# Top-k softmax with the exponentials taken before the comparison, FFN weights kept unsplit, and a shorter list of early expert work

## The chip, the cores and the metric

One NeuronCore of a Trainium2 chip runs the whole program. The metric is the time of one execution in device microseconds; it was measured three times before the change.

## The reference, cut to what matters

```python
def _attn_ref(q, k, v):                       # 2 batches, 8 heads, 576 tokens, head size 64
    scores = scale * np.matmul(q, k.transpose(0, 1, 3, 2))
    kth = np.partition(scores, -32, axis=-1)[..., -32:-31]
    scores = np.where(scores >= kth, scores, -1000000000.0)
    attn = np.exp(scores - np.max(scores, axis=-1, keepdims=True))
    attn = attn / (np.sum(attn, axis=-1, keepdims=True) + 1e-09)
    return np.matmul(attn, v)

def _moe_ref(x, w_in, w_out):                 # 1152 tokens, 512 wide, 2048 hidden
    h = x @ w_in
    return (h * (1.0 / (1.0 + np.exp(-h)))) @ w_out

def _moe2_ref(x, w_gate, w1, w2):             # 8 experts, 1024 hidden, all of them on all tokens
    P = np.exp(x @ w_gate - (x @ w_gate).max())
    for _ in range(8):                        # Sinkhorn: rows, then columns, normalised
        ...
    for e in range(8):
        out += P[:, e:e+1] * (np.maximum(x @ w1[e], 0.0) @ w2[e])
```

The output of the attention feeds the first FFN, and that feeds the experts. The first FFN's weights arrive as 64-bit floats.

## The kernel before, in words

**Tiles.** The 1152 tokens are nine token tiles of 128, numbered 0 to 8. The attention is done in five groups of token tiles: [0], [1, 2], [3, 4], [5, 6], [7, 8]. A group is made of units, one or two for each of the four head pairs. A unit has score tiles of 128 queries by 576 keys: one for each head and query block, and "h" tiles in which half of the rows belong to one head and half to the other. There are 72 score tiles (64 and 8 h).

**A score tile** (`score_tile`, L276). Four matmuls of 288 columns: two with the high part of q against all 128 rows of `kk` (which holds the high and the low part of k), two with the low part of q against the 64 rows that hold k's high part. ACT copies the scores to `s`. VectorE then finds the 32 largest of each row: four MAX8 (L295) with three MATCH_REPLACE8 (L300) between them. ACT computes Relu(kth - s) (L303), VectorE overwrites what lies below the kth with a large negative number (COPY_PREDICATED, L304), ACT takes the exponential with its row sum (L305), VectorE forms the reciprocal of the sum (L306, L307), and GpSimd scales the row (L308). TensorE transposes the row (L311, L313) and multiplies with v (L322).

**The FFN on one tile or two.** Group g's tokens go through the first FFN as m0 (tile 0), m1 (tiles 1, 2), m2 (tiles 3, 4), and m3 (tiles 5 to 8, after all attention). m1 to m3 run over 16 blocks f of 128 hidden values. A block computes `hidden` (12 matmuls), the activation, and `product` (six matmuls of 512 columns with two token tiles), each value in a high and a low part of reduced 32-bit precision, three matmuls for each full product. In m1 and m2 the activation after ACT's tanh (L398) is four GpSimd instructions: t (L402), g (L403), gH (L416), gL (L417). m0 works with whole 32-bit weights in four blocks of 512.

**Splitting.** A weight block of 128 by 512 is split by one ACT copy (L127) and one subtraction (L128), on GpSimd unless said otherwise. While m0 runs, each of its 32 weight blocks is converted from 64 bits (`narrow`, L444 to L449), split once, and written to HBM in split form (`kept_in`, `kept_out`); m1 to m3 load the split form and need no split.

**Early expert work.** The eight experts on nine token tiles are 72 pieces. The list `FILL` has some of them done early, between the FFN's parts: after m0 five experts on tile 0, after m1 experts 0 and 1 on tiles [1, 2], after m2 expert 2 on [1, 2] and experts 0 and 1 on [3, 4]. These results go to HBM and are added later. "split" treats each of an expert's eight blocks as above, "half" splits only the first weight and runs the product in one whole 32-bit pass, "split+half" alternates. What is left runs after the Sinkhorn iterations, in units of up to four token tiles.

**What sets the order.** Each instruction gets a priority (`tc.cur_priority`; units of the attention count up in steps of GAP), and a scheduler puts every engine's instructions in one fixed order at build time. The engines and the DMA queue of SP then run in that order. Buffers are shared by pools: three `wa` and four `wb` weight tiles (`wap`, `wbp`), five score tiles (`SB`). Groups 2 and 4 put their attention output into the same `x` tile, groups 1 and 3 into another.

## Time and profile before

| | us |
|---|---|
| three runs | 1337.5, 1337.9, 1342.37 (median 1337.9) |
| the profiled execution | 1342.67 |
| its span, first to last instruction | 1340.8 |

| engine | busy us | share of the span |
|---|---|---|
| TensorE (PE) | 1263.8 | 94% |
| VectorE (DVE) | 703.5 | 52% |
| ScalarE (ACT) | 552.5 | 41% |
| GpSimd (POOL) | 428.0 | 32% |

The shares are means over unlike stages. The attention lasts until the last reciprocal at 522.5 us; in that time VectorE is nearly always at work. From then to about 613 us the rest of the early expert work runs, with m3 from 591 us. From 690 us on TensorE runs experts alone. PE's busy time counts matmuls that overlap, so a PE that is busy all of the time may still be working at less than its best pace; the distance from one start to the next tells the pace.

### The profile page before, as it was taken

To read this page: it belongs to the slowest core of one execution; us is meant where nothing else is said; L and a number is where in the kernel's file an instruction comes from. 1 tells how busy PE (TensorE), PEld (TensorE's weight loads), DVE (VectorE), ACT (ScalarE), POOL (GpSimd) and SP (SyncE) were. 2 spreads that over 40 slices of the span, in tenths; PEclk is the share of its full clock that TensorE was granted. 3 is DMA by queue.
4 is the path that set the end of the run, shared out by engine and by line. 5 is a ranking of instruction groups with operands and counts; after the bars stand their busy time and mean duration, and the time that the engine had idled before them with its cause. 6 is when DMAs were issued, how large, how long until landed. Compare 5 with 4: busy or idle time off the path is not lost.

```text
span 1340.8 us, 18725 instructions
## 1 busy us (share of the span) xinstructions
PE 1263.8 (94%) x6563; PEld 994.6 (74%) x6563; DVE 703.5 (52%) x1489; ACT 552.5 (41%) x1169; POOL 428.0 (32%) x475
## 2 busy tenths in 40 slices
PE   3579989999999999989999999999999999999998
PEld 2344545578768887768979879889888888888887
DVE  5999989989999985022233541232231331323332
ACT  4879745655667566542231231131131221313221
POOL 2768411146557787970010130020020110202110
PEclk9979889999899999999999999999999999999999
DMA  6999977797445864577520250040030120313210
GB/s 172 274 316 333 289 245 223 226 291 242 131 122 165 290 211 120 149 242 251 187 72 8 67 162 0 7 119 1 16 118 0 47 79 9 104 31 113 76 33 32
DMA packets 159725, 186.91 MB, mean 139 GB/s; under 512 B 34320, under 2 KB 110864, under 8 KB 159632
## 3 DMA queue, kind: packets, MB, share of 16 engines
q1 hardware_dynamic: 159632, 185.72, 44.8%
q8 instruction: 52, 0.85, 0.3%
q14 instruction: 41, 0.34, 0.1%
HBM read 153.63 MB, written 23.07 MB: 132 GB/s over the span
## 4 chain that ended last, share of the span: by engine, by line
PE 53%; DMA 2%; POOL 2%; issue 1%; DVE 1%; ACT 0%; DVEq 0%; SPq 0%; ACTq 0%; POOLq 0%
PE h L135 9%; PE h L137 9%; PE h L136 9%; PE y L135 7%; PE y L137 7%; PE y L136 7%; DMA yk<-ky 1%; PE bank L137 1%; PE bank L135 1%; PE bank L136 1%; POOL wa L128 1%; PE y_m L136 1%; PE y_m L137 1%; PE y_m L135 1%; POOL wb L128 1%
## 5 line engine op out<-in xcount | busy, mean ns | idle before, releaser
L410 ACT ACTIVATE gH<-h 128x512 fp32r<-128x512 f32 (+2 forms) x144 | 73.4, 510 | 384.4 <-PE h L137 381.8
L411 DVE SCALAR_TENSOR_TENSOR gL<-h,gH 128x512 fp32r<-128x512 f32 (+2 forms) x144 | 83.3, 578 | 278.2 <-ACT gH L410 278.1
L128 POOL TENSOR_TENSOR wc<-raw,wc 128x512 fp32r<-128x512 f32 x40 | 52.2, 1305 | 404.6 <-ACT wc L127 404.6
L295 DVE MAX8 m<-w 128x8 f32<-128x576 f32 x192 | 141.6, 749 | 0.4
L128 POOL TENSOR_TENSOR wa<-raw,wa 128x512 fp32r<-128x512 f32 x64 | 82.9, 1295 | 148.5 <-ACT wa L127 146.4
L137 PE MATMUL h<-x1H,wc 128*128 128x512 f32 (+2 forms) x360 | 124.8, 347 | 0.0
L136 PE MATMUL h<-x1L,wc 128*128 128x512 f32 (+2 forms) x360 | 124.8, 347 | 0.0
L135 PE MATMUL h<-x1H,wc 128*128 128x512 f32 (+2 forms) x360 | 124.4, 346 | 0.0
L128 DVE TENSOR_TENSOR wc<-raw,wc 128x512 fp32r<-128x512 f32 x40 | 51.5, 1288 | 120.2 <-ACT wc L127 115.8
L135 PE MATMUL y<-wc,gH 128*128 128x512 f32 x285 | 111.7, 392 | 0.0
L136 PE MATMUL y<-wc,gH 128*128 128x512 f32 x285 | 111.6, 391 | 0.0
L137 PE MATMUL y<-wc,gL 128*128 128x512 f32 x285 | 101.9, 392 | 0.6 <-DVE gL L411 0.6
L300 DVE MATCH_REPLACE8 w<-m,w 128x576 f32<-128x576 f32 x128 | 95.1, 743 | 0.0
L308 POOL TENSOR_SCALAR s<-s,sm 128x576 f32<-128x576 f32 x64 | 47.8, 748 | 104.4 <-DVE sm L307 64.6
L137 PE MATMUL h<-x1H,wa 128*128 128x512 f32 (+2 forms) x216 | 75.2, 348 | 0.0
L135 PE MATMUL h<-x1H,wa 128*128 128x512 f32 (+2 forms) x216 | 75.1, 348 | 0.0
L136 PE MATMUL h<-x1L,wa 128*128 128x512 f32 (+2 forms) x216 | 75.0, 347 | 0.0
L135 PEld LDWEIGHTS h<-x1H,wc 128*128 128x128 f32 x360 | 67.7, 188 | 9.5
L136 PEld LDWEIGHTS h<-x1L,wc 128*128 128x128 f32 x360 | 67.8, 188 | 9.5
L127 ACT ACTIVATE wc<-raw 128x512 fp32r<-128x512 f32 x80 | 46.5, 623 | 65.5 <-PE y L137 45.4
L137 PEld LDWEIGHTS h<-x1H,wc 128*128 128x128 f32 x360 | 67.7, 188 | 7.4
L136 PE MATMUL y<-wb,gH 128*128 128x512 f32 x171 | 67.7, 396 | 0.0
(228 smaller groups left out, 3196.7 us busy)
## 6 DMA issues: line engine op xcount, KB each, us to landing
raw<-in_moe_w_dram SPq DMA_DIRECT2D x196, 256.0 KB, 3.0
wa<-kept_in SPq DMA_DIRECT2D x48, 512.0 KB, 4.3
...
```

Source lines behind the costliest of these rows:

```text
L127: nc.scalar.activation(dH, src, AF.Copy)
L128: eng.tensor_sub(dL, src, dH.bitcast(F32))
L135: nc.tensor.matmul(ps, wH, xH, start=first, stop=False)
L136: nc.tensor.matmul(ps, wH, xL, start=False, stop=False)
L137: nc.tensor.matmul(ps, wL, xH, start=False, stop=last)
L295: nc.vector.max(mr, src)
L300: nc.vector.match_replace(out=w, in_to_replace=mr, in_values=src, imm_value=-3e38)
L308: nc.gpsimd.tensor_scalar(s, s, sm[:, 3:4], 1.0, op0=ALU.mult, op1=ALU.mult)
L410: nc.scalar.activation(gH, ph, AF.Relu)
L411: nc.vector.scalar_tensor_tensor(gL, ph, 0.0, gH.bitcast(F32), op0=ALU.max, op1=ALU.subtract)
```

## The change

The top-k softmax takes the exponential of the whole row into a new tile `e` right after the first MAX8 (the maximum is known then). After the fourth MAX8 one VectorE instruction compares the scores with the kth, multiplies the result with `e`, and gives the row sum. The Relu on ACT, the COPY_PREDICATED and the row sum of the exponential go.

The low part of q is kept in two buffers `qLz` of which the rows of the other head are zero, so that all four matmuls of a score tile have 128 rows; the last chunk of keys of the product with v is likewise 128 rows with zeros in v.

m0's weights are written to HBM as they are (`kept_in`, `kept_out`, half the bytes); all 32 blocks stay in buffers of their own until then. m1, m2 and m3 load them and split them, two splits for a block f: on GpSimd, in m3 the second one on VectorE. The pools `wap` and `wbp` now lie where m0's buffers were.

`FILL` loses expert 2 on [1, 2] and expert 1 on [3, 4]; expert 1 on [1, 2] becomes "split+half".

```diff
-    1: [(0, [1, 2], "half"), (1, [1, 2], "split")],
-    2: [(2, [1, 2], "split+half"), (0, [3, 4], "split"), (1, [3, 4], "split")],
+    1: [(0, [1, 2], "half"), (1, [1, 2], "split+half")],
+    2: [(0, [3, 4], "split")],
...
-    return conv_at(i) + 2 * GAP
+    return conv_at(i) + 4 * GAP
...
-    kept_in = drp.tile([DFF // P, P, 2 * W], F32, name="kept_in")
-    kept_out = drp.tile([DFF, 2 * W], F32, name="kept_out")
+    kept_in = drp.tile([DFF // W, NDC, P, W], F32, name="kept_in")
+    kept_out = drp.tile([DFF, W], F32, name="kept_out")
...
-        nc.sync.dma_start(vn[0:64, :, 4, :], vs[:, 4 * P : S, :].rearrange("h p d -> p h d"))
+        nc.gpsimd.memset(vn[0:64, :, 4, :], 0.0)
+        nc.sync.dma_start(vn[64:P, :, 4, :], vs[:, 4 * P : S, :].rearrange("h p d -> p h d"))
...
+            if n:
+                nc.sync.dma_start(low.bitcast(F32)[r, j, : n * P], qL.bitcast(F32)[r, : n * P])
...
-            low = (qL[r, cols], kk[r]) if len(heads) == 1 else (qL[:, j, cols], kk)
-            for a, c, part in ((qq[:, j, cols], kk, 0), (*low, 1)):
+            for part, a in enumerate((qq, qL)):
...
-                nc.vector.tensor_scalar(sm[:, 0:1], m8[:, 0:1], MASKED, -SCALE,
-                                        op0=ALU.max, op1=ALU.mult)
+                nc.vector.tensor_scalar(sm[:, 0:1], m8[:, 0:1], -SCALE, None, op0=ALU.mult)
+                nc.scalar.activation(e, s, AF.Exp, scale=SCALE, bias=sm[:, 0:1])
...
-        nc.scalar.activation(w, s, AF.Relu, scale=-1.0, bias=m8[:, TOPK - 1 : TOPK])
-        nc.vector.copy_predicated(s, w.bitcast(I32), neg.to_broadcast([P, S]))
-        nc.scalar.activation(s, s, AF.Exp, scale=SCALE, bias=sm[:, 0:1], accum_out=sm[:, 1:2])
+        nc.vector.scalar_tensor_tensor(s, s, m8[:, TOPK - 1 : TOPK], e, op0=ALU.is_ge, op1=ALU.mult,
+                                       accum_out=sm[:, 1:2])
...
-            ws = (wap, wbp)[part].tile([P, 2 * W], F32R, name=f"wab_{i}", tag=("wa", "wb")[part])
-            split(ws[:, 0:W], ws[:, W:], x)
-            if part:
-                nc.sync.dma_start(kept_out[r], ws.bitcast(F32))
...
+            tc.cur_priority = keep_at(i)
+            nc.sync.dma_start(kept_out[r] if part else kept_in[F, c], x)
...
-        nc.sync.dma_start(ws[0].bitcast(F32), kept_in[f])
-        r = slice(f * P, (f + 1) * P)
-        nc.sync.dma_start(ws[1].bitcast(F32), kept_out[r])
+        a = kept_in[f // NDC][:, :, f % NDC * P : (f % NDC + 1) * P].rearrange("c p f -> p c f")
+        load_split(ws[0], a, nc.gpsimd)
+        load_split(ws[1], kept_out[f * P : (f + 1) * P], nc.vector if late else nc.gpsimd)
```

Three places in the engines' fixed order follow. In the rows a name before the arrow is written, names behind it are read; the first number after `t_m2_`, `g_m2_`, `gH_m2_`, `gL_m2_` is the block f.

GpSimd in the middle of m2, from one block's t to that of the block after next, before:

```order
L402 TENSOR_TENSOR t_m2_10_4336<-t_m2_10_4336,hs_m2_10_4338 128x256
L417 TENSOR_TENSOR gL_m2_9_4301<-g_m2_9_4302,gH_m2_9_4300 128x256
L403 TENSOR_TENSOR g_m2_10_4335<-t_m2_10_4336,hs_m2_10_4338 128x256
L416 TENSOR_SCALAR gH_m2_10_4333<-g_m2_10_4335 128x256
L308 TENSOR_SCALAR s_4_1_2_0_0_6334<-s_4_1_2_0_0_6334,sm_4_1_2_0_0_6338 128x576
L417 TENSOR_TENSOR gL_m2_10_4334<-g_m2_10_4335,gH_m2_10_4333 128x256
L402 TENSOR_TENSOR t_m2_11_4369<-t_m2_11_4369,hs_m2_11_4371 128x256
L403 TENSOR_TENSOR g_m2_11_4368<-t_m2_11_4369,hs_m2_11_4371 128x256
L416 TENSOR_SCALAR gH_m2_11_4366<-g_m2_11_4368 128x256
L417 TENSOR_TENSOR gL_m2_11_4367<-g_m2_11_4368,gH_m2_11_4366 128x256
L402 TENSOR_TENSOR t_m2_12_4402<-t_m2_12_4402,hs_m2_12_4404 128x256
```

and the same place after:

```order
L407 TENSOR_TENSOR t_m2_10_4377<-t_m2_10_4377,hs_m2_10_4379 128x256
L408 TENSOR_TENSOR g_m2_9_4337<-t_m2_9_4338,hs_m2_9_4340 128x256
L422 TENSOR_TENSOR gL_m2_8_4297<-g_m2_8_4298,gH_m2_8_4296 128x256
L128 TENSOR_TENSOR wa_262_4508<-raw_263_4510,wa_262_4508 128x512
L421 TENSOR_SCALAR gH_m2_9_4335<-g_m2_9_4337 128x256
L128 TENSOR_TENSOR wb_250_4392<-raw_252_4397,wb_250_4392 128x512
L408 TENSOR_TENSOR g_m2_10_4376<-t_m2_10_4377,hs_m2_10_4379 128x256
L407 TENSOR_TENSOR t_m2_11_4416<-t_m2_11_4416,hs_m2_11_4418 128x256
L128 TENSOR_TENSOR wb_254_4431<-raw_256_4436,wb_254_4431 128x512
L422 TENSOR_TENSOR gL_m2_9_4336<-g_m2_9_4337,gH_m2_9_4335 128x256
L128 TENSOR_TENSOR wa_266_4547<-raw_267_4549,wa_266_4547 128x512
L421 TENSOR_SCALAR gH_m2_10_4374<-g_m2_10_4376 128x256
```

Two splits of 128 by 512 now stand between one block's t and the next one's, and gL comes a block later.

ACT after the last block of m2, where group 4's attention output `xH_4` is taken out of PSUM (`pav`) and the last three score tiles (`s_4_1_3_0_1` is the first of them) follow, before:

```order
L398 ACTIVATE t_m2_15_4501<-bank2_136 128x256
L401 ACTIVATE hs_m2_15_4503<-bank2_136 128x256
L131 ACTIVATE xH_4_5989<-pav_4_1_0_6140 128x256
L131 ACTIVATE xH_4_5989<-pav_4_1_1_6302 128x256
L127 ACTIVATE wa_215_4592<-raw_216_4594 128x512
L305 ACTIVATE s_4_1_3_0_0_6481,sm_4_1_3_0_0_6485<-s_4_1_3_0_0_6481,sm_4_1_3_0_0_6485 128x576
L127 ACTIVATE wa_219_4626<-raw_221_4628 128x512
L325 ACTIVATE aT_4_1_2_0_6327<-pt_4_1_2_0_0_6353 128x4x128
L326 ACTIVATE aT_4_1_2_0_6327<-pt2_4_1_2_0_0_6358 64x128
L288 ACTIVATE s_4_1_3_0_1_6514<-ps_4_1_3_0_1_6509 128x576
```

and after:

```order
L403 ACTIVATE t_m2_15_4572<-bank2_134 128x256
L406 ACTIVATE hs_m2_15_4574<-bank2_134 128x256
L131 ACTIVATE xH_4_5552<-pav_4_1_0_5705 128x256
L131 ACTIVATE xH_4_5552<-pav_4_1_1_5869 128x256
L127 ACTIVATE wa_279_4670<-raw_280_4672 128x512
L127 ACTIVATE wb_271_4615<-raw_273_4620 128x512
L330 ACTIVATE aT_4_1_2_0_5896<-pt_4_1_2_0_0_5922 128x4x128
L331 ACTIVATE aT_4_1_2_0_5896<-pt2_4_1_2_0_0_5927 128x128
L293 ACTIVATE s_4_1_3_0_1_6083<-ps_4_1_3_0_1_6078 128x576
```

In both, the last three score tiles come after the last block of m2; the exponential (L305) that stood among them before has moved ahead.

SP's DMA queue at the first loads of expert weights (`wa_10` to `wb_13`), before:

```order
L472 DMA kept_out_76<-wab_29_1006 128x1024
L476 DMA kept_in_75<-wab_27_981 128x4x128
L487 DMA wa_10_1131<-in_moe2_w1_dram 128x2x512
L269 DMA qq_0_0_3_1893<-qH_0_0_3_1894 64x128 x3
L476 DMA kept_in_75<-wab_27_981 128x4x128
L269 DMA qq_0_0_3_1893<-qH_0_0_3_1894 64x128
L273 DMA qL_half0_125<-qL_0_0_3_1892 64x64 x2
L488 DMA wb_12_1133<-in_moe2_w2_dram 128x2x512
L487 DMA wa_11_1132<-in_moe2_w1_dram 128x2x512
L488 DMA wb_13_1134<-in_moe2_w2_dram 128x2x512
```

and after:

```order
L274 DMA qq_0_0_3_1802<-qH_0_0_3_1803 64x128 x4
L278 DMA qLz0_121<-qL_0_0_3_1804 64x128
L278 DMA qLz1_122<-qL_0_1_3_3205 64x128
L197 DMA kn_1_3_3666<-in_k_dram 128x4x64 x2
L244 DMA qn_1_2_0_3436<-in_q_dram 64x2x64
L198 DMA kn_1_3_3666<-in_k_dram 64x2x64
L484 DMA wa_10_1034<-in_moe2_w1_dram 128x2x512
L485 DMA wb_12_1036<-in_moe2_w2_dram 128x2x512
L484 DMA wa_11_1035<-in_moe2_w1_dram 128x2x512
```

The loads now stand behind two writes of `qLz`, one buffer for every second unit; the second of them overwrites what the score tiles of the last unit of group 1 read.

## Rows read from the trace of the kernel before

**Rows 1.** Busy us of each engine (count), PE clock, DMA share, GB/s, by stretch:

```profile
40.00:160.00 120.00, 95.61 (x382) 54.70 (x383) 116.95 (x275) 100.47 (x210) 87.48 (x77) 0.89 0.98 310
278.00:346.00 68.00, 67.57 (x454) 54.78 (x453) 58.30 (x136) 39.98 (x108) 44.99 (x68) 1.00 0.81 259
346.00:434.00 88.00, 85.18 (x503) 63.62 (x502) 82.74 (x200) 60.65 (x134) 51.80 (x60) 0.96 0.45 133
434.00:496.00 62.00, 61.55 (x390) 50.83 (x389) 56.12 (x133) 36.89 (x90) 46.77 (x70) 1.00 0.78 258
550.00:575.00 25.00, 20.72 (x126) 17.50 (x124) 0.00 (x0) 11.68 (x25) 25.00 (x29) 1.00 0.60 168
```

**Rows 2.** Timeline of ACT: first tanh of m1, last of m2, end of m3:

```profile
278.34 0.38 ACT L398 ACTIVATE t_m<-bank 128x256 f32<-128x256 f32 x1
...
495.65 0.38 ACT L398 ACTIVATE t_m<-bank 128x256 f32<-128x256 f32 x1 [0.15 <-PE bank L137]
...
689.63 0.60 ACT L560 ACTIVATE x<-bank 128x512 f32<-128x512 f32 x1 [1.47 <-PE bank L137]
```

**Rows 3.** GpSimd's groups within m2, 434 to 496 us (busy us, mean ns):

```profile
L402 POOL TENSOR_TENSOR t_m<-t_m,hs_m 128x256 f32<-128x256 f32 x15 | 11.1, 740 | 12.8 <-ACT hs_m L401 12.8
...
L417 POOL TENSOR_TENSOR gL_m<-g_m,gH_m 128x256 fp32r<-128x256 f32 x14 | 10.4, 742 | 0.7
L308 POOL TENSOR_SCALAR s<-s,sm 128x576 f32<-128x576 f32 x9 | 6.7, 749 | 0.2 <-ACT yo L672 0.2
L416 POOL TENSOR_SCALAR gH_m<-g_m 128x256 fp32r<-128x256 f32 x14 | 5.7, 405 | 0.9
L128 POOL TENSOR_TENSOR wa<-raw,wa 128x512 fp32r<-128x512 f32 x2 | 2.6, 1286 | 0.0
```

**Rows 4.** Timeline of GpSimd where it is never idle (start, duration):

```profile
557.44 1.30 POOL L128 TENSOR_TENSOR wb<-raw,wb 128x512 fp32r<-128x512 f32 x1
558.69 1.30 POOL L128 TENSOR_TENSOR wa<-raw,wa 128x512 fp32r<-128x512 f32 x1
```

**Rows 5.** Timeline of ACT: first evictions of late expert units and their successors:

```profile
1003.19 0.60 ACT L410 ACTIVATE gH<-h 128x512 fp32r<-128x512 f32 x1 [2.17 <-PE h L137]
...
1047.72 0.60 ACT L410 ACTIVATE gH<-h 128x512 fp32r<-128x512 f32 x1 [4.96 <-PE h L137]
...
1179.21 0.39 ACT L410 ACTIVATE gH<-h 128x256 fp32r<-128x256 f32 x1 [0.81 <-PE h L137]
...
1204.50 0.60 ACT L410 ACTIVATE gH<-h 128x512 fp32r<-128x512 f32 x1 [3.78 <-PE h L137]
```

**Rows 6.** Groups by line and shape, whole span (busy us, mean ns):

```profile
L304 DVE COPY_PREDICATED_SCALAR s<-w,neg 128x576 f32 x64 | 55.4, 866 | 5.6 <-ACT w L303 4.7 <-PE bank L137 0.9
L128 DVE TENSOR_TENSOR wc<-raw,wc 128x512 fp32r<-128x512 f32 x40 | 51.5, 1288 | 120.2 <-ACT wc L127 115.8 <-DMA wa<-kept_in 3.6 <-PE h L137 0.8
L772 DVE SCALAR_TENSOR_TENSOR acc<-y,pr,acc 128x512 f32<-128x512 f32 x39 | 27.2, 743 | 11.7 <-PE y L137 11.7
L128 DVE TENSOR_TENSOR wb<-raw,wb 128x512 fp32r<-128x512 f32 x24 | 16.6, 692 | 51.5 <-ACT wb L127 51.5
L305 ACT ACTIVATION_READ_ACCUMULATOR s<-s,sm 128x1 f32 x64 | 12.5, 196 | 0.0
```

**Rows 7.** Timeline of VectorE and of GpSimd at 771 us:

```profile
771.21 1.17 DVE L772 SCALAR_TENSOR_TENSOR acc<-yk,pr,acc 128x512 f32<-128x512 f32 x1 [0.78 <-DMA yk<-ky]
...
770.54 1.30 POOL L128 TENSOR_TENSOR wc<-raw,wc 128x512 fp32r<-128x512 f32 x1 [4.14 <-ACT wc L127]
```

**Rows 8.** Timeline of PE: score matmuls with 64 and with 128 rows:

```profile
331.88 0.53 PE L285 MATMUL ps<-kk,qL 64*128 64x288 f32 x2
332.34 0.50 PE L135 MATMUL bank<-wb,gH_m 128*128 128x512 f32 x1
...
225.25 0.42 PE L285 MATMUL ps_h<-kk,qL_half 128*128 128x288 f32 x2
225.52 0.42 PE L285 MATMUL ps_h<-kk,qq_half 128*128 128x288 f32 x2
```

More of the change, by code (lines that the diff above doesn't have):

```diff
@@ L34 @@
 RAWB = 4
-WF = 22
 WA = 3
@@ L185, in topk_attention_moe_sinkhorn_kernel @@
     qL_half = [qtp.tile([P, 2, P], F32R, name=f"qL_half{i}", tag=f"qL_half{i}", bufs=1) for i in range(2)]
-    for t in qq_half + qL_half:
+    qLz = [qtp.tile([P, 2, 2 * P], F32R, name=f"qLz{i}", tag=f"qLz{i}", bufs=1) for i in range(2)]
+    for t in qq_half + qL_half + qLz:
         nc.gpsimd.memset(t.bitcast(F32), 0.0)
     half_no = [0]
+    full_no = [0]
     def load_kv(b, p):
@@ L251, in turn_q @@
             nc.tensor.transpose(pq[:, n * P : w], qn[0:64, 1, :, :].rearrange("p h d -> p (h d)"), ident[0:64, 0:64])
-        qL = qtp.tile([P, 2 * P], F32R, name=f"qL_{b}_{p}_{t0}", tag="qL")
+        low = qLz[full_no[0] % 2]
+        full_no[0] += n > 0
         qq = qtp.tile([P, 2, 2 * P], F32R, name=f"qq_{b}_{p}_{t0}", tag="qq") if n else None
@@ L258, in turn_q @@
                     nc.scalar.activation(qq[o : o + 64, j, :w], pq[r, :w], AF.Copy)
-                nc.vector.tensor_sub(qL[r, :w], pq[r, :w], qq[r, j, :w].bitcast(F32))
-            return qq, qL, None
+                nc.vector.tensor_sub(low[r, j, :w], pq[r, :w], qq[r, j, :w].bitcast(F32))
+            return qq, low, None
         qH = qtp.tile([P, 2 * P], F32R, name=f"qH_{b}_{p}_{t0}", tag="qH")
+        qL = qtp.tile([P, 2 * P], F32R, name=f"qL_{b}_{p}_{t0}", tag="qL")
         evac_split(qH[:, :w], qL[:, :w], pq[:, :w])
@@ L291, in score_tile @@
         sm = small.tile([P, 4], F32, name=f"sm_{nm}", tag="sm")
+        e = sp.tile([P, S], F32, name=f"e_{nm}", tag="e")
         src = s
@@ L311, in score_tile @@
             nc.tensor.transpose(pt[:, c, :], s[:, c * P : (c + 1) * P], ident)
-        pt2 = ps_t.tile([64, P], F32, name=f"pt2_{nm}", tag="tr")
-        nc.tensor.transpose(pt2, s[:, 4 * P : S], ident)
+        pt2 = ps_t.tile([P, P], F32, name=f"pt2_{nm}", tag="tr")
+        nc.tensor.transpose(pt2, s[:, S - P : S], ident)
         return pt, pt2
@@ L459, in first_blocks @@
             cols = slice(F * W, (F + 1) * W) if part == 0 else slice(0, W)
-            x = cvp.tile([P, W], F32, name=f"wf_{i}", tag="wf", bufs=WF)
+            x = cvp.tile([P, W], F32, name=f"wf_{i}", tag=f"wf{i}", bufs=1)
             if w_in.dtype == F32:
@@ L467, in first_blocks @@
             got.append(x)
-            tc.cur_priority = split_at(i)
-            ws = (wap, wbp)[part].tile([P, 2 * W], F32R, name=f"wab_{i}", tag=("wa", "wb")[part])
-            split(ws[:, 0:W], ws[:, W:], x)
-            if part:
-                nc.sync.dma_start(kept_out[r], ws.bitcast(F32))
-                continue
-            for h in range(2):
-                to = kept_in[F * NDC : (F + 1) * NDC, :, h * W + c * P : h * W + (c + 1) * P]
-                nc.sync.dma_start(to.rearrange("n p f -> p n f"),
-                                  ws.bitcast(F32)[:, h * W : (h + 1) * W].rearrange("p (n f) -> p n f", f=P))
+            tc.cur_priority = keep_at(i)
+            nc.sync.dma_start(kept_out[r] if part else kept_in[F, c], x)
         return lambda F: (got[2 * NDC * F : 2 * NDC * F + NDC], got[2 * NDC * F + NDC : 2 * NDC * (F + 1)])
@@ L647, in topk_attention_moe_sinkhorn_kernel @@
                 row_ffn("m0", x0, banks[0], banks[1], blocks, DFF // W, True, hp)
+            wap = right.enter_context(tc.tile_pool(name="wap", bufs=WA, side="right", reuse_waits="tile"))
+            wbp = right.enter_context(tc.tile_pool(name="wbp", bufs=WB, side="right", reuse_waits="tile"))
             late = right.enter_context(tc.tile_pool(name="late", bufs=1, side="right", reuse_waits="tile"))
@@ L698, in topk_attention_moe_sinkhorn_kernel @@
     ffn("m3", [(*xs[3], slice(0, 2 * P)), (*xs[4], slice(0, 2 * P))], ys,
-        lambda f, m: kept_weights(f), DFF // P, True, hidB, hpB, late=True, depth=1)
+        lambda f, m: kept_weights(f, True), DFF // P, True, hidB, hpB, late=True, depth=1)
     tc.cur_priority = uid() * 100
```

16 lines of the change are left out of this document (6 added, 10 removed).

## The prediction

> **What bounds the kernel now.** I read the stretches first. Through m1 (278 to 346 us) and m2 (434 to 496 us) TensorE is busy without a gap, VectorE some nine tenths and GpSimd two thirds to three quarters of the time [rows 1]; m1 starts and m2 ends where the tanh rows stand [rows 2]. So TensorE and VectorE are both close to full in the attention, and GpSimd has a quarter to a third left. Past the attention the picture turns: from 550 to 575 us GpSimd is busy in all 25 us while PE has gaps [rows 1]. That is the last early expert work, which waits for its splits. After the expert units begin, TensorE alone counts; there a unit of four token tiles takes 1047.72 - 1003.19 = 44.5 us and one of two 1204.50 - 1179.21 = 25.3 us [rows 5]. I work along this chain: up to m1, m1, the stretch between m1 and m2, m2, from m2 to the end of m3, and the late units. All of it stands against the profiled execution, 1342.67 us (span 1340.8 and 1.9 us around it); the median of the runs is 4.8 us lower, so I apply the difference to 1337.9.
>
> **Late units: +44.5 us.** Two pieces of early work go, each two token tiles of one expert. Expert 2's late unit of two tiles becomes one of four, 44.5 - 25.3 = +19.2. Expert 1 gets one of two more, +25.3 [rows 5]. Nothing hides this, as TensorE is the limit there. Four saved results fewer are added; that was beside matmuls, nothing.
>
> **m1 and m2: +13 and +16 us.** GpSimd's order now has two weight splits in each block. A split starts 1.25 us after the one before it, 0.05 less than its duration, when GpSimd is never idle [rows 4]; I take 0.05 off the others too: t, g and gL 0.69 each, gH 0.36, the scaling of a score row 0.70 [rows 3]. Between the first and the last t of m1 the order has 15 t, 14 g, 14 gH, 13 gL, 29 splits and 13 scalings: 42 x 0.69 + 14 x 0.36 + 29 x 1.25 + 13 x 0.70 = 79.4 us. In m2 there are 15, 15, 14, 13, 28 and 10: 76.7 us. The stretches are 68 and 62 us now, so GpSimd, with room before, becomes the limit of both. With 1.5 us each for results not yet there I take 81 and 78. Lower end: the plain sums; upper end: 5 us more each. ACT's two copies per block lie beside 40 of 68 busy us [rows 1] and a Relu and an accumulator read less, nothing.
>
> **The new VectorE step.** COPY_PREDICATED cost 0.866 us [rows 6]. The nearest row to its successor is the scalar_tensor_tensor of 512 columns, 0.743 [rows 6]; in proportion 576 columns are 0.84 at most. It also returns a sum, which the trace of before shows on VectorE nowhere; ACT's read of its accumulator takes 0.196 [rows 6], so this costs 0 to 0.2 and I take 0.1, half way, since a shorter ACT step would do it too. Beside an idle GpSimd the step then costs 0.94, +0.07 for a score tile (-0.03 to +0.17). Beside a busy one it is longer: with both tensors in SBUF the same instruction took 1.17 us while a GpSimd split ran [rows 7], 0.43 over its 0.743, and VectorE's own subtraction takes 1.288 in the chunks where GpSimd subtracts too, 0.692 in those where it doesn't [rows 6]. So +0.4 to +0.6 where GpSimd is full; I take 0.5 times its busy share. What goes is the wait for ACT's Relu, 4.7 us over all tiles [rows 6].
> In m1 that is 13 tiles. Eleven tiles took VectorE 58.3 busy us now [rows 1], 5.3 each; 13 x (5.3 + 0.57) = 76, under the 81 of GpSimd, so it is hidden there, as in m2. Between m1 and m2 (88 us now) VectorE is busy for 82.7 [rows 1], and 14 tiles at 0.07 + 0.5 x 0.6 add 5: 88, just the length. TensorE gains there by the next point, so I take **+2** (0 to +10).
>
> **Up to m1: -6 us.** The pair of score matmuls with 64 rows holds PE for 332.34 - 331.88 = 0.46 us, one with 128 rows 225.52 - 225.25 = 0.27 [rows 8]; with the change of form at the pair's start, 0.3 us for a score tile that isn't h. Ten such tiles lie between the first expert block and m1: -3. From 40 to 160 us the DMA engines are full (0.98), ACT at 100 and GpSimd at 87 of 120 us [rows 1]; 32 splits and half of the kept bytes leave that stretch, so m0 can end earlier. But the expert loads now stand in SP's queue behind a write to `qLz1`, which waits for the score matmuls of the second tile of group 1's last unit, and behind them are the expert blocks on TensorE. So most of m0's gain waits there, and I take another -3. Bounds: -20, if all of the traffic's gain comes through, to +10, if the loads come a whole score tile late. The zeros for v and qLz are set before they are needed, nothing.
>
> **From the last tanh of m2 to the end of m3: -58 us.** Now 689.63 - 495.65 = 194 us [rows 2]. After: about 10 us of GpSimd's queue and the last product, 5 for the new token tiles and the first hidden block of expert 0 on [3, 4], then 7 blocks at GpSimd's pace, 2 x 1.25 + 0.36 + 0.69 = 3.55 [rows 3, 4], 25 us; the last three score tiles and their output run beside these. Then 7 us for the last products and m3's first hidden block, and m3: a block of four token tiles is a late unit's block, 44.5 / 8 = 5.56, times 16 = 89. Together 136. Of 58 us saved, some 45 are the removed pieces, the rest the starved stretch that went with them [rows 1].
>
> **Sum.** -6 + 13 + 2 + 16 - 58 + 44.5 = +11.5 us: 1349 against the median of 1337.9.
>
> **Rivals.**
> The accumulating step runs at half pace. Against it: the trace has no sum on VectorE, so nothing denies it. The bound is twice 0.84 with the read, 1.78, +0.91 for a tile. Then the stretch between m1 and m2 takes 82.7 + 14 x 0.91 = 95.5 (+5.5 over mine), m1 13 x 6.2 = 81 stays, the tiles before m1 (VectorE busy 117 of 120 [rows 1]) are some 10 us later, the last three 3: +30 in all, 1368. Chance 0.14. The Trainium skill speaks for this rival: "Vector Engine (DVE) Microarchitecture Reference", section "Points that are easy to get wrong", says that this instruction with two SBUF sources that aren't bf16 runs at half throughput, with no port left for the accumulator. By that rule it would be this rival's time; by the row without a sum [rows 7] two 32-bit sources alone do not halve it.
> GpSimd loses what VectorE takes. If each new step held GpSimd for its 0.84 us, m1, m2 and the last tiles (22) would cost 18 us more, as GpSimd sets their pace: 1367. Against it: the split at 770.54 kept its 1.30 us while the other ran from 771.21 [rows 7]. Chance 0.09. The Trainium skill, "SBUF — State Buffer", section "Who interferes with whom", calls the shared port pair an exclusive lock, with the later one fully blocked. The row differs: locked out until 771.84, the step would have ended at 772.6, not 772.38.
> Not slower: the start pays for the splits. If m0, freed of 32 splits and 8 MB of writes, hands its lead on through the expert blocks, m1 begins up to 20 us earlier than 278.34 [rows 2], 14 more than I took, and GpSimd's sums hold without their 3 us: -6, 1332; with the middle stretch carried by the shorter score matmuls, 1330. It decides from m1's first tanh before about 266. For it: the full DMA engines [rows 1]. Against it: the queue order, and VectorE at 117 of 120 us, which sets when score tiles come. Chance 0.27.
>
> **How the numbers follow.** The forecast with its own bounds (1340 to 1360) has 0.42, of this 0.14 below 1344.6; the two slower rivals 0.23; the rival that isn't slower 0.27, half of it below 1331.2; a late start of the expert blocks beyond my bound, slower, 0.08. Half a per cent is about what a measurement of this kernel can tell from no change. Faster 0.13 and a little of the forecast's lower end, 0.15; the same 0.27; slower 0.58. The range runs from the sum with the start's lower bound and the other terms at their lower ends (11.5 - 14 - 3 - 2 - 4 for the end = -11.5, 1326) to the half pace with a late start (1374).
>
> **What would show it.** First tanh of m1 near 272, its last near 353; GpSimd's busy share in both blocks near 1 and PE's pace falling; last tanh of m2 near 521, m3's end near 657, then the late units 44 us longer. Right steps also show in the new VectorE row: 0.84 alone, 1.2 to 1.4 beside splits. If GpSimd has idle time in m1, or the sum's step is above 1.6 with GpSimd idle, the forecast's reasons are wrong.

## The result and the profile after

The changed kernel takes 1353.62 us (median of four, 1352.55 to 1354.54) against 1339.62 us before: 1.0092 times as long, with a 95% interval of 1.0065 to 1.0120. The profiled execution has a span of 1352.7 us, 11.9 more than before. The sum of the prediction was +11.5. That the two are so close is partly luck, as the stretches show. The marks are ACT's rows as in [rows 2], in the changed kernel these (start, duration):

```profile
259.27 0.38 ACT L403 ACTIVATE t_m<-bank 128x256 f32<-128x256 f32 x1
...
343.97 0.37 ACT L403 ACTIVATE t_m<-bank 128x256 f32<-128x256 f32 x1
...
432.17 0.38 ACT L403 ACTIVATE t_m<-bank 128x256 f32<-128x256 f32 x1
...
513.29 0.39 ACT L403 ACTIVATE t_m<-bank 128x256 f32<-128x256 f32 x1 [1.99 <-PE bank L137]
...
659.34 1.09 ACT L557 ACTIVATE x<-bank 128x512 f32<-128x512 f32 x2 [1.47 <-PE bank L137]
```

They are the first and last tanh of m1, the first and last of m2, and the end of m3. Between them:

| stretch | before, us | after, us | change | forecast |
|---|---|---|---|---|
| up to m1's first tanh | 278.3 | 259.3 | -19.0 | -6 |
| m1 | 67.8 | 84.7 | +16.9 | +13 |
| m1's end to m2's start | 88.3 | 88.2 | -0.1 | +2 |
| m2 | 61.3 | 81.1 | +19.8 | +16 |
| m2's last tanh to m3's end | 194.0 | 146.0 | -48.0 | -58 |
| late expert units | 651.2 | 693.4 | +42.2 | +44.5 |

The two FFN stages and the stretch between, in the columns of [rows 1]:

```profile
259.30:344.00 84.70, 75.60 (x545) 60.53 (x541) 83.42 (x205) 55.71 (x137) 84.26 (x97) 1.00 0.49 135
344.00:432.20 88.20, 81.30 (x487) 61.40 (x486) 88.20 (x217) 51.78 (x110) 53.82 (x57) 0.98 0.43 125
432.20:513.30 81.10, 62.99 (x352) 48.80 (x351) 51.78 (x122) 39.78 (x86) 81.10 (x95) 0.92 0.35 105
```

The fifth busy number is GpSimd's: it is busy for 84.26 of 84.7 us in m1 and for all of m2. In m1 VectorE, the third number, is just as full (83.42); in m2 it has 29 us to spare. TensorE, without a gap in both stages before, now has 9 and 18 us of them.

The groups of the new instructions, and of GpSimd's splits (busy us, mean ns):

```profile
L310 DVE SCALAR_TENSOR_TENSOR s<-s,m,e 128x576 f32<-128x576 f32 x64 | 70.3, 1098 | 0.5
L310 DVE DVE_READ_ACCUMULATOR s<-s,m,e 128x1 f32 x64 | 5.0, 78 | 0.0
L128 POOL TENSOR_TENSOR wa<-raw,wa 128x512 fp32r<-128x512 f32 x96 | 128.6, 1340 | 127.7 <-ACT wa L127 120.6 <-DMA wa<-in_moe_w_dram 2.3 <-issue 1.7
```

The new VectorE step takes 1.098 us on the mean and its sum's read 0.078, where COPY_PREDICATED took 0.866 [rows 6]. The mean hides two cases. In the timeline of VectorE (first fence) one step runs while GpSimd is idle, three while it is at work (second fence, GpSimd's rows at those three):

```profile
183.55 0.80 DVE L310 SCALAR_TENSOR_TENSOR s<-s,m,e 128x576 f32<-128x576 f32 x1
...
300.20 1.28 DVE L310 SCALAR_TENSOR_TENSOR s_h<-s_h,m_h,e_h 128x576 f32<-128x576 f32 x1
...
305.77 1.23 DVE L310 SCALAR_TENSOR_TENSOR s<-s,m,e 128x576 f32<-128x576 f32 x1
...
371.88 1.44 DVE L310 SCALAR_TENSOR_TENSOR s<-s,m,e 128x576 f32<-128x576 f32 x1
```

```profile
300.83 1.81 POOL L128 TENSOR_TENSOR wa<-raw,wa 128x512 fp32r<-128x512 f32 x1
...
305.65 0.73 POOL L407 TENSOR_TENSOR t_m<-t_m,hs_m 128x256 f32<-128x256 f32 x1
306.35 1.79 POOL L128 TENSOR_TENSOR wa<-raw,wa 128x512 fp32r<-128x512 f32 x1
...
371.43 1.28 POOL L128 TENSOR_TENSOR wa<-raw,wa 128x512 fp32r<-128x512 f32 x1
```

Each side can make the other longer: these steps take 1.2 to 1.4 us instead of 0.80, and two of the splits 1.8 instead of 1.30 [rows 4]. Over the whole trace, the 20 steps that no GpSimd instruction overlaps average 0.803 us, the 28 that are overlapped all through 1.286; the 27 splits that overlap a step by more than 0.6 us average 1.52 us, the 149 that hardly do 1.29.

These means mix two cases, for the step and GpSimd take turns. The split at 371.43 came first: it took its usual 1.28 us, and the step waited and ended 0.61 us after it. All 38 steps that begin during a GpSimd instruction with more than 0.2 us to go end 0.60 to 0.62 us after it, whether they take 0.81 us or 1.86. The splits at 300.83 and 306.35 came second: they end 1.16 and 1.14 us after the step, as do (1.13 to 1.17) 14 of the 16 splits that begin during a step; in the other two cases the step was itself still waiting. So whichever comes second waits for the first but for an overlap of some 0.2 us (0.80 - 0.61, 1.29 - 1.14), and a split loses some 0.5 us to a step that came before it and nothing to one that came after.

### The profile page after: what moved, and what is told of

Its sections match the earlier page's. It is cut to its first block, busy times and chain, and to the rows that moved or that the text cites. A ratio compares the mean times of both kernels' runs of the same rounds, so it can differ in the third digit from the quotient of the medians.

```text
span 1352.7 us, 18344 instructions
## 1 busy us (share of the span) xinstructions
PE 1247.3 (92%) x6467; PEld 992.8 (73%) x6467; DVE 734.8 (54%) x1585; ACT 515.8 (38%) x1045; POOL 446.0 (33%) x469
## 4 chain that ended last, share of the span: by engine, by line
PE 68%; DVE 14%; DMA 6%; issue 4%; POOL 4%; ACT 2%; SPq 1%; DVEq 0%; POOLq 0%; ACTq 0%
PE h L137 9%; PE h L136 9%; PE h L135 9%; PE y L135 8%; PE y L136 8%; PE y L137 8%; DVE m L301 5%; DVE w L307 5%; PE bank L497 3%; PE bank L504 2%; DMA wfr<-in_moe_w_in_dram 2%; DVE s L310 2%; PE bank L137 2%; PE bank L136 1%; PE bank L135 1%
## 5 line engine op out<-in xcount | busy, mean ns | idle before, releaser
L416 DVE SCALAR_TENSOR_TENSOR gL<-h,gH 128x512 fp32r<-128x512 f32 (+2 forms) x152 | 88.9, 585 | 311.2 <-ACT gH L415 311.0
L128 POOL TENSOR_TENSOR wa<-raw,wa 128x512 fp32r<-128x512 f32 x96 | 128.6, 1340 | 127.7 <-ACT wa L127 120.6
L136 PE MATMUL h<-x1L,wc 128*128 128x512 f32 (+2 forms) x380 | 132.7, 349 | 0.0
L137 PE MATMUL h<-x1H,wc 128*128 128x512 f32 (+2 forms) x380 | 132.7, 349 | 0.0
L135 PE MATMUL h<-x1H,wc 128*128 128x512 f32 (+2 forms) x380 | 132.3, 348 | 0.0
L135 PE MATMUL y<-wc,gH 128*128 128x512 f32 x305 | 119.5, 392 | 0.0
L136 PE MATMUL y<-wc,gH 128*128 128x512 f32 x305 | 119.4, 391 | 0.0
L137 PE MATMUL y<-wc,gL 128*128 128x512 f32 x305 | 109.4, 391 | 0.0
L127 ACT ACTIVATE wb<-raw 128x512 fp32r<-128x512 f32 x84 | 53.0, 631 | 71.7 <-PE y L137 23.6
L137 PE MATMUL h<-x1H,wa 128*128 128x512 f32 (+2 forms) x228 | 80.0, 351 | 0.0
L135 PE MATMUL h<-x1H,wa 128*128 128x512 f32 (+2 forms) x228 | 79.8, 350 | 0.0
L135 PEld LDWEIGHTS h<-x1H,wc 128*128 128x128 f32 x380 | 71.5, 188 | 10.5
L136 PEld LDWEIGHTS h<-x1L,wc 128*128 128x128 f32 x380 | 71.5, 188 | 10.4
L137 PEld LDWEIGHTS h<-x1H,wc 128*128 128x128 f32 x380 | 71.5, 188 | 8.3
L136 PE MATMUL y<-wb,gH 128*128 128x512 f32 x183 | 72.5, 396 | 0.0
```

The lines of the kernel that those rows point to most:

```text
L127: nc.scalar.activation(dH, src, AF.Copy)
L128: eng.tensor_sub(dL, src, dH.bitcast(F32))
L135: nc.tensor.matmul(ps, wH, xH, start=first, stop=False)
L136: nc.tensor.matmul(ps, wH, xL, start=False, stop=False)
L137: nc.tensor.matmul(ps, wL, xH, start=False, stop=last)
L416: nc.vector.scalar_tensor_tensor(gL, ph, 0.0, gH.bitcast(F32), op0=ALU.max, op1=ALU.subtract)
```

## The experiments

The stretches of every kernel, read from the same rows of ACT; in brackets the score tiles that VectorE had finished by m1's first tanh. Times are medians; s9 and s12 are single runs. Kernels that are alike up to m1 (the changed one, s3, s5, s6, s8, s9) differ there by up to 4 us from one profile to the next, 257.8 to 261.5.

| kernel | us | to m1 (tiles) | m1 | to m2 | m2 | to m3's end | late |
|---|---|---|---|---|---|---|---|
| before | 1339.6 | 278.3 (36) | 67.8 | 88.3 | 61.3 | 194.0 | 651.2 |
| after | 1353.6 | 259.3 (33) | 84.7 | 88.2 | 81.1 | 146.0 | 693.4 |
| s1 | 1341.0 | 270.5 (35) | 67.9 | 88.3 | 58.3 | 202.1 | 651.7 |
| s2 | 1347.1 | 264.8 (33) | 83.0 | 85.2 | 74.7 | 144.1 | 693.4 |
| s3 | 1359.5 | 260.2 (33) | 84.6 | 86.2 | 84.1 | 192.8 | 650.7 |
| s4 | 1342.5 | 294.2 (38) | 63.6 | 89.8 | 51.4 | 145.6 | 693.6 |
| s5 | 1349.0 | 260.7 (33) | 85.7 | 90.1 | 76.8 | 145.6 | 693.3 |
| s6 | 1328.5 | 257.8 (33) | 88.7 | 84.3 | 55.2 | 142.9 | 693.3 |
| s7 | 1325.3 | 267.5 (33) | 84.4 | 83.7 | 53.5 | 141.5 | 693.7 |
| s8 | 1320.9 | 261.5 (33) | 83.7 | 83.1 | 55.6 | 142.2 | 693.9 |
| s9 | 1337.5 | 258.9 (33) | 68.5 | 87.0 | 84.1 | 141.6 | 694.9 |
| s10 | 1331.9 | 265.4 (33) | 83.4 | 87.4 | 56.1 | 144.1 | 693.4 |
| s11 | 1349.1 | 298.7 (37) | 64.8 | 83.0 | 52.3 | 198.5 | 650.2 |
| s12 | 1354.5 | 281.8 (43) | 79.2 | 88.0 | 69.3 | 141.1 | 693.4 |

My theory was that GpSimd's splits set m1 and m2, that the shorter list about pays for itself, and that the new softmax costs where GpSimd is full. The rivals were VectorE as the limit (by its number of tiles or by the new step), and the wait for ACT that the new softmax saves.

### s1: the new softmax alone

```diff
 # the kernel before
-WF = 22
+WF = 20
...
+        e = sp.tile([P, S], F32, name=f"e_{nm}", tag="e")
...
+                nc.scalar.activation(e, s, AF.Exp, scale=SCALE, bias=sm[:, 0:1])
...
-        (Relu, COPY_PREDICATED, exponential with row sum)
+        nc.vector.scalar_tensor_tensor(s, s, m8[:, TOPK - 1 : TOPK], e, op0=ALU.is_ge, op1=ALU.mult,
+                                       accum_out=sm[:, 1:2])
```

> The kernel before with the new softmax alone (20 instead of 22 buffers for m0's weights, to make room for the new tile). Theory (the new step costs VectorE 0.80 us beside an idle GpSimd and 1.29 beside a busy one, where COPY_PREDICATED took 0.86 beside either, and it lengthens the GpSimd instruction beside it by 0.2 to 0.4): what VectorE limits gets longer, up to m1 by 3 to 8 us (36 tiles), between m1 and m2 by 2 to 5 (14 tiles); m1 and m2, which TensorE limits here, stay at 68 and 61 to 64. Time 1339.6 + 5 to 12, some 1347. Rival (the wait for ACT's Relu is worth more than the step's price): up to m1 5 us less, 1330 to 1336.

1341.0 us, 0.9991 times the kernel before (0.9966 to 1.0017): no difference. Neither theory nor rival gave the time. Up to m1 it is 7.8 us faster, which is the rival's gain; from m2's last tanh to m3's end it is 8.1 slower, which neither had; at m2's last tanh two score tiles fewer are done (66 instead of 68), and they come later; that this is the cause wasn't tested. What the gain is shows in the waits of VectorE in the first 277 us. Before (us, times, longest):

```profile
DVE sm L306 <- ACT s L305: 4.6, 1, 4.6
...
DVE s L304 <- ACT w L303: 1.3, 3, 0.6
```

In s1 nothing stands in their place, and VectorE is idle for 9.3 us instead of 16.3 between 30 us and its 36th tile. The exponential and the Relu, which it had to wait for on an ACT that was busy 100 of 120 us [rows 1], come off its path.

### s2: the changed kernel with the old softmax

```diff
 # the changed kernel
-                nc.scalar.activation(e, s, AF.Exp, scale=SCALE, bias=sm[:, 0:1])
...
-        nc.vector.scalar_tensor_tensor(s, s, m8[:, TOPK - 1 : TOPK], e, ...)
+        nc.scalar.activation(w, s, AF.Relu, scale=-1.0, bias=m8[:, TOPK - 1 : TOPK])
+        nc.vector.copy_predicated(s, w.bitcast(I32), neg.to_broadcast([P, S]))
+        nc.scalar.activation(s, s, AF.Exp, scale=SCALE, bias=sm[:, 0:1], accum_out=sm[:, 1:2])
```

> The changed kernel with the softmax of the kernel before (Relu, COPY_PREDICATED, exponential with row sum). Theory: in m1 and m2 GpSimd stays the limit, but 9 to 13 of its instructions are no longer lengthened, so m1 goes from 84.7 to about 80 and m2 from 81.1 to about 77; between m1 and m2, where VectorE is busy for all 88 us, 14 tiles get 0.25 us shorter, 88 to about 85; up to m1 0 to 5 us less. Time 1353.6 - 12 = 1342. Rival (GpSimd's own number of splits sets m1 and m2, and the old step's wait for ACT gives back what its VectorE time saves): within 3 us of 1353.6.

1347.1 us, 1.0049 times the kernel before (1.0033 to 1.0064). So the rest of the change costs about half a per cent by itself, and the softmax 6.5 us on top, where it costs nothing in the kernel before. It begins m1 5.5 us later (waits for ACT's Relu and exponential are back, 6.8 us of VectorE's time), and is 1.7, 3.0 and 6.4 us faster in m1, between m1 and m2, and in m2, where the new step stands beside GpSimd. The mechanism held: these three stages give 11.1 of the 12 us expected of them. The time moved by half of the 12 forecast because the start, expected to be 0 to 5 us shorter, is 5.5 longer; the rival (within 3 us) fell. GpSimd's busy time (the fifth) in m1 and m2 goes from 84.26 and 81.10 down to:

```profile
264.80:347.80 83.00, 74.20 (x518) 59.96 (x515) 78.82 (x192) 63.80 (x160) 78.42 (x99) 0.98 0.48 131
...
433.00:507.70 74.70, 60.32 (x352) 46.45 (x351) 43.76 (x105) 45.81 (x105) 74.34 (x92) 0.95 0.39 113
```

In m2 the stage follows GpSimd down by as much. In m1 GpSimd now has 4.6 us idle, and m1 hardly gets shorter: a first hint that m1 has a second limit.

### s3: the old list of early work

```diff
 # the changed kernel
-    1: [(0, [1, 2], "half"), (1, [1, 2], "split+half")],
-    2: [(0, [3, 4], "split")],
+    1: [(0, [1, 2], "half"), (1, [1, 2], "split")],
+    2: [(2, [1, 2], "split+half"), (0, [3, 4], "split"), (1, [3, 4], "split")],
```

> The changed kernel with the list of early expert work of the kernel before (expert 2 on [1, 2] and expert 1 on [3, 4] early again, expert 1 on [1, 2] with all blocks split). The late part, 693.4 us now, goes back to 651. Theory (the early pieces are limited by GpSimd's splits, so the list was shortened at no loss): the stretch from the last tanh of m2 to the end of m3 grows from 146 by 42 to 55 us, and the stretch between m1 and m2 by up to 5: 1353 to 1370, most likely 1361. Rival (TensorE's idle time at 500 to 550 us takes up part of the early work): it grows by 30, 1342.

1359.5 us. The late part is 42.7 us shorter, the stretch before it 46.8 longer, as the theory had it (42 to 55); the rival's 30 fell. After m2's last tanh the windows show GpSimd (fifth) busy for 84 of 93 us and TensorE (first) with 7 us of gaps, before m3 starts:

```profile
515.10:608.30 93.20, 86.17 (x537) 71.42 (x538) 21.47 (x51) 48.81 (x104) 84.39 (x94) 1.00 0.50 147
```

The shorter list is worth 6 us, the difference of two terms of over 40 each.

### s4: weights split in m0 and kept in split form

```diff
 # the changed kernel
-            tc.cur_priority = keep_at(i)
-            nc.sync.dma_start(kept_out[r] if part else kept_in[F, c], x)
+            (split and writes of the split form, as before)
...
-        load_split(ws[0], a, nc.gpsimd)
-        load_split(ws[1], kept_out[f * P : (f + 1) * P], nc.vector if late else nc.gpsimd)
+        nc.sync.dma_start(ws[0].bitcast(F32), kept_in[f])
+        nc.sync.dma_start(ws[1].bitcast(F32), kept_out[r])
...
+WF = 18
```

> The changed kernel with the weights of the first FFN split in m0 and kept in split form, as in the kernel before (18 instead of 32 buffers for m0's weights, which is what fits beside the new tiles): the new softmax, the 128-row score matmuls and the short list stay. Theory (the splits on GpSimd make m1 and m2 longer, and the traffic and splits in m0 make the start longer): m1 back from 84.7 to 66 to 72 us, m2 from 81.1 to 60 to 66, the first tanh of m1 back from 259 to 272 to 285, from the last tanh of m2 to the end of m3 some 136 to 146. Time 1353.6 - 15 - 17 + 20 - 5 = about 1337. Rival (VectorE with the new step limits m1 and m2 just as well: 13 tiles of 5.9 us are 77 us): m1 and m2 stay over 75, and the time goes to 1355 to 1370.

1342.5 us, 11 less than the changed kernel. m1 falls to 63.6 us and m2 to 51.4, so both are long with the splits and short without. It is less clean than it looks: 10 and 4 score copies of ACT lie in them here, 13 and 6 in the changed kernel, so VectorE has less to do beside them too. The start is 35 us later, more than I thought: with 18 buffers and the traffic of the split form, m1 begins at 294.2, after 38 score tiles instead of 33. The stretch to m3's end stays at 145.6, though the 16 + 16 splits of m3 are gone: they don't set it. The splits of expert 0 on [3, 4], early in that stretch, are still there.

### s5: one GpSimd instruction of each block moved to ACT

```diff
 # the changed kernel
-            nc.gpsimd.tensor_scalar(gH, g, 1.0, 0.0, op0=ALU.mult, op1=ALU.add)
+            nc.scalar.activation(gH, g, AF.Copy)
```

> The changed kernel with one GpSimd instruction of each block of m1 and m2 (gH, the copy of g into the reduced type) done by ACT instead; nothing else. Theory (GpSimd's queue sets the length of both): 14 instructions of 0.41 to 0.45 us go from each, so m1 from 84.7 to about 79 and m2 from 81.1 to about 75, time 1353.6 - 11 = 1342. Rival (in m1 VectorE, busy for 83.4 of 84.7 us, is as much the limit, so only m2 gains): m1 84, m2 75, time 1347.

The edit also moves this instruction of the early experts' split blocks, 12 of 0.41 us, outside m1 and m2; the stretches where they lie aren't shorter for it (90.1 and 145.6 us). 1349.0 us, about the rival's time; the profiled execution is the longest of its ten, 1354.6. m2 is 4.3 us shorter, m1 not at all (85.7). So in m1 GpSimd wasn't alone: the window shows it with 5.7 us idle, and VectorE (third) still at 82 of 85.7:

```profile
260.70:346.40 85.70, 74.91 (x514) 62.30 (x510) 81.97 (x194) 56.57 (x145) 80.01 (x85) 0.94 0.48 133
```

### s6: the low parts kept by m1

m1 splits as in the changed kernel and writes each low part to HBM; m2 and m3 load it, so that only ACT's copy is left there.

```diff
 # the changed kernel
+    kept_low = drp.tile([DFF // P, 2, P, W], F32, name="kept_low")
...
+        for i, src in enumerate((a, kept_out[f * P : (f + 1) * P])):
+            low = kept_low[f, i]
+            if g == 1:
+                load_split(ws[i], src, nc.gpsimd)
+                nc.sync.dma_start(low, ws[i].bitcast(F32)[:, W:])
+                continue
+            raw = rwp.tile([P, W], F32, name=f"raw_{uid()}", tag="raw")
+            nc.sync.dma_start(raw.rearrange("p (c f) -> p c f", f=P) if i == 0 else raw, src)
+            nc.sync.dma_start(ws[i].bitcast(F32)[:, W:], low)
+            nc.scalar.activation(ws[i][:, 0:W], raw, AF.Copy)
```

> The changed kernel, where m1 writes the low part of each split to HBM (256 KB for each of 32 weight blocks), and m2 and m3 load it beside the whole weights, so that ACT's copy is all that is left of the split there; nothing else. Theory: m1 stays at 84 to 88, m2 loses 28 of GpSimd's splits (38 of 81 us) and falls to what TensorE needs, 52 to 60, from the last tanh of m2 to the end of m3 some 138 to 146: time 1353.6 - 21 to 32, most likely 1327, below both kernels. Rival (16 more writes and reads in SP's queue, each behind a split or a free buffer, hold up the loads behind them): m1 95 or m2 over 70, time 1345 or more.

1328.5 us, 0.9893 times the kernel before (0.9864 to 0.9922) and 25 us below the changed one. m2 falls from 81.1 to 55.2 us, and TensorE (first) is full there again, at DMA engines 0.89 busy:

```profile
430.80:486.00 55.20, 53.87 (x356) 45.50 (x354) 47.68 (x122) 37.89 (x85) 49.11 (x67) 1.00 0.89 275
```

m1 is 4 us longer with its 8 MB of writes, 88.7 where 84 to 88 was given. The score tiles beside m2 are as many as in the changed kernel (59 done at its start, 69 at its end), so this shows most cleanly that GpSimd's splits set m2.

### s7, s8, s10: the same with the old softmax, with gH on ACT, and with both

```diff
 # s7: s6 with the diff of s2; s8: s6 with the diff of s5; s10: s6 with both
+            nc.scalar.activation(gH, g, AF.Copy)
```

> As the run with the low parts kept by m1, with the softmax of the kernel before. Theory (with GpSimd no longer the limit of m2, the new step's price there is gone, and what it saves in VectorE's waits up to m1 counts): the first tanh of m1 5 us later than with the new softmax, m1 2 us shorter, the stretch to m2 3 us shorter, m2 alike: within 4 us of that run. Rival (the old softmax stays 6 us better, as it is in the changed kernel): 6 us or more below it.

> As the run with the low parts kept by m1 (new softmax), with gH of m1 and m2 on ACT too. Theory: m1 another 5 us shorter than in that run, m2 within 2 us of it, as GpSimd isn't its limit any more: 5 us below it, some 1322. Rival (VectorE is the limit of m1): within 2 us of it.

> As the run with the low parts kept by m1 and gH on ACT, with the softmax of the kernel before. Theory (with GpSimd relieved the new step's price and the waits for ACT that it saves are about even): within 4 us of 1321. Rival (the old softmax stays 6 us better, as in the changed kernel): 1315 or less; or, as ACT now has gH too, its waits count more: 1327 or more.

s7 takes 1325.3 us (0.9867, 0.9841 to 0.9892): with m2 no longer GpSimd's, the two softmaxes are within 4 us, as expected. In the profiles its start is 9.7 us later than s6's, and the rest 7.6 shorter. s8 takes 1320.9 us, the best of all: 0.9836 times the kernel before (0.9808 to 0.9864), below both kernels. m1 is 5 us shorter than in s6, as the theory had it, but begins 3.7 later. In the profiles s8 is 2.2 us below s6, in the medians 7.6; the intervals touch, so its lead over s6 isn't settled. s10 takes 1331.9 us (0.9901, 0.9869 to 0.9934), some 11 above s8: its third expectation holds. With gH on ACT as well, the old softmax has VectorE wait: it is idle for 20.2 us up to its 36th tile, against 15.7 in s8.

### s9: one split less for each block of m1

The low part of the second weight is not formed in m1.

```diff
 # the changed kernel, m1 only
+            nc.scalar.activation(ws[1][:, 0:W], raw, AF.Copy)
+            return ws[0], (ws[1][:, 0:W], ws[1][:, 0:W])
```

> The changed kernel with one split a block in m1 instead of two: the low part of the second weight is left out there, and its high part is multiplied in its place, so every matmul stays. GpSimd has 16 x 1.4 = 22 us less to do in m1. Measure: the time from 30 us to the last tanh of m1, by score tile finished until then (after: 314 us for 45 tiles, 6.98; before 7.18; with gH on ACT 7.03). Theory (VectorE's score tiles set the time up to the end of m1, with or without splits on GpSimd beside them): 6.8 to 7.1 again. Rival (GpSimd sets m1): 17 us come off at the same tiles, 6.6 or less. The length of m1 alone doesn't tell, as fewer score tiles stand in the order beside it (10 instead of 13).

Up to m1's last tanh 297.4 us for 43 tiles, 6.92 each: the theory's value. Yet m1 is 16 us shorter, and the whole 1337.5 us, 16 less. The order at build time changed with the work: 10 score tiles stand between the tanh rows of m1 instead of 13. The three that moved are done beside m2, where VectorE has time. GpSimd's work in m1 fell too, to 64.0 us, so s9 doesn't tell how much of the 16 us either of them gives. The row of m1:

```profile
258.90:327.40 68.50, 66.20 (x497) 55.97 (x492) 64.90 (x162) 48.51 (x125) 64.00 (x81) 1.00 0.57 159
```

So "6.9 us for a tile" told nothing of what m1's length costs. My reading, which no run separates from GpSimd's shorter list: VectorE fixes when the score tiles are done, the order fixes how many of them m1 has to wait for, and GpSimd's splits in m1 raise that number.

### s11: the 128-row forms alone

```diff
 # the kernel before
+    qLz = [qtp.tile([P, 2, 2 * P], F32R, name=f"qLz{i}", tag=f"qLz{i}", bufs=1) for i in range(2)]
...
-            low = (qL[r, cols], kk[r]) if len(heads) == 1 else (qL[:, j, cols], kk)
-            for a, c, part in ((qq[:, j, cols], kk, 0), (*low, 1)):
+            for part, a in enumerate((qq, qL)):
```

> The kernel before with the 128-row forms alone (qLz, zeros in v; 20 instead of 22 buffers for m0's weights). The prediction's step: a score tile takes TensorE 0.3 us less, some 3 us up to m1 and as much in m1 (where TensorE is the limit) and in m2: 1340 - 6 to 9 = 1332. Rival (VectorE sets the time up to m2's start, so only m2's part is left): 1337 to 1340.

1349.1 us, 1.0046 times the kernel before (1.0023 to 1.0069): slower, where theory and rival had it faster or equal. m1 and m2 are 3 and 9 us shorter, but m1 begins 20 us later. TensorE's waits between 100 and 300 us:

```profile
PE bank L513 <- DMA wa<-in_moe_w_dram: 8.0, 3, 4.6
PE bank L506 <- DMA wb<-in_moe_w_dram: 7.3, 2, 4.7
```

It waits 15.3 us for weights of the early expert rows; before it was 5.9 us. SP's queue in turn waited 5.1 us in three waits at such loads (L493) for score matmuls. This is the prediction's last rival, the late start of the expert blocks; it came true in this kernel, not in the changed one, where these waits are 2.3 us. The 20 buffers aren't the cause, since s1 has them too; how much of the 20 us the queue explains beyond those waits stays open.

### s12: a top 24

One MAX8 and one MATCH_REPLACE8 of the seven search steps are left out.

```diff
 # the changed kernel
-TOPK = 32
+TOPK = 24
```

> The changed kernel with a top 24 instead of a top 32: one MAX8 and one MATCH_REPLACE8 of seven are left out, 0.744 + 0.738 = 1.48 us of VectorE's time for a score tile; the rest of the work is alike. Measure: time from 30 us to the last tanh of m1 and to the first tanh of m2, by score tile finished until then (after: 6.98 and 6.82). Theory (VectorE sets the time up to m2's first tanh): 5.4 to 5.8 at both. Rival (TensorE, GpSimd and the loads set it, and VectorE is only busy beside them): over 6.3.

The same time as the changed kernel, 1354.5 us, with 107 us less work for VectorE (72 x 1.48). By tile it is 5.85 us at m1's first tanh, 6.24 at m1's last and 6.16 at m2's first: between theory and rival, so both fall as stated. The order now puts 44 score tiles ahead of m1's first tanh (36 in the changed kernel) and 69 ahead of m2's (63), and m1 begins 22 us later for it. The windows of m1 and m2:

```profile
281.80:361.00 79.20, 66.29 (x413) 51.56 (x412) 50.61 (x125) 45.69 (x105) 77.93 (x91) 0.98 0.38 107
...
448.90:518.20 69.30, 50.53 (x274) 40.37 (x272) 0.90 (x3) 30.32 (x68) 69.06 (x84) 0.95 0.39 114
```

With VectorE (third) at 51 of 79 us and GpSimd (fifth) at 78, m1 is down to GpSimd's own work. m2, with VectorE idle, is all GpSimd's: 69.3 us, with one row scaling where the changed kernel has ten. So m1 had two limits close together: GpSimd's 79 us, and 13 score tiles on VectorE, 83 to 85. They aren't independent: in the changed kernel's m1 the 13 steps take 16.5 us instead of 13 x 0.80 = 10.4, and GpSimd's instructions beside them 6.6 us more than alone. Each engine's busy time there holds some 6 us of waiting for the other.

## Why the prediction was right, and where it was not

The sum held: +11.5 against +11.9 in the profiles and +14.0 in the medians. But two terms were off by 13 and 10 us and two more by 4, and they cancel.

**Late units, +44.5.** Right: +42.2, and -42.7 back in s3. Nothing hid them.

**From m2's last tanh to m3's end, -58.** It was -48.0. The reason, early pieces whose cost about equals what they save late, is shown by s3. The size failed in two steps. I gave 15 us to GpSimd's queue, the last product and the first new block of expert 0; the first eviction of that block comes 21.3 us after m2's last tanh. In that gap TensorE waits 3 us for the new token tiles and then runs at half pace (last section). And I took m3 as 89 us with 7 ahead; 2.6 us after expert 0's eighth eviction comes m3's first tanh, and from there to its end it takes 98.6, TensorE busy nearly throughout. The blocks of expert 0 themselves came as forecast, 23.5 us from the first eviction to the eighth (25). A late unit's block was the wrong row to price m3 by, for in the kernel before it took 98.2 us too, from this row to its end at 689.63 [rows 2]:

```profile
591.42 0.60 ACT L398 ACTIVATE t_m<-h 128x512 f32<-128x512 f32 x1 [0.23 <-PE h L137]
```

**m2, +16.** Right in its reason: GpSimd is busy for all 81.1 us, and the stage falls to 55.2 in s6, where the splits go. The size, +19.8, was short because I gave a split 1.25 us after [rows 4] and the others 0.05 less than in [rows 3]; the splits in m2 average 1.34 us, 1.286 where no step runs beside them. In all, GpSimd's instructions there wait 4.7 us for the nine steps; with nine row scalings of 0.75 that is nearly the 11.8 us by which s12, without steps in m2, is shorter.

**m1, +13.** The length came out as forecast (+16.9), the reason only by half. The step that failed is the count behind "11 tiles took 58.3 us, 5.3 each". Eleven is what the order shows between the tanh rows; VectorE's work runs behind it, and the trace has 37 MAX8 there, 9.25 tiles, so a tile costs 6.3 us. After, it is 83.42 us for 12.75 tiles, 6.5 each, where I had 76. VectorE was the other limit (s5), GpSimd's 79 us, with ten score tiles beside it, a close second (s12).

**Up to m1, -6.** It was -19.0, near the lower bound of -20. Two steps failed. I held that the expert loads wait behind `qLz`'s writes; in the changed kernel TensorE waits 2.3 us for them (15.3 in s11). And I took what goes with ACT's Relu as 4.7 us over all tiles [rows 6]; the new softmax takes 5 to 8 us of waits off VectorE in this stretch alone (s1, s2), since the exponential's sum goes with it. Without the softmax the start gains 13.5 (s2), and with the split form kept it is 35 us later than in the changed kernel (s4, whose 18 buffers have an unknown part in that). How the gain divides between splits, traffic and buffers stays open.

**m1's end to m2's start, +2.** Right (-0.1). VectorE is busy for all 88.2 us; the new step's price there is 3.0 us by s2.

**The new step.** 0.80 us alone (forecast 0.84), 1.29 on the mean beside GpSimd (1.2 to 1.4, but single ones up to 1.94), 0.078 for the sum's read (0.1): right. The rows that gave these were the same instruction without a sum, alone and beside a split [rows 6, 7].

**The rivals.** Half pace with the sum (1.78 us with the read): it fell, as the 0.80 shows. The Trainium skill's rule behind it, "Vector Engine (DVE) Microarchitecture Reference", section "Points that are easy to get wrong", speaks of half throughput for two such sources; the trace doesn't agree, with 0.80 us for 576 columns where MAX8 takes 0.744 to 0.746 with one source. GpSimd locked out for the whole step: its mechanism came true, its size did not. The two do take turns, but a GpSimd instruction that came first loses nothing and a split that came second some 0.5 us, not 0.84; by s2 the whole price of the step in m1 and m2 is 8.1 us, where this rival had 18 with the last tiles. The row held against it [rows 7] was misread: the step there ended 0.54 us after the split, which is the same turn, with 0.2 us of its 0.743 overlapped. The Trainium skill, "SBUF — State Buffer", section "Who interferes with whom", says that a VectorE instruction with two SBUF inputs contends with GpSimd reading SBUF, and calls what they contend for an exclusive lock; the trace agrees, with all 38 steps ending 0.60 to 0.62 us after the GpSimd instruction that they began beside, but for that overlap. The start pays for the splits: its sign came true up to m1 (259.3, before the 266 it named), but its other half, GpSimd's bare sums, did not, and the time is 14 us above before. What the start gained was paid to m1: up to m1's last tanh the changed kernel is 2.1 us ahead, with 45 tiles done instead of 44.
